# Sliding-window attention and MLP, two layers on one core: 164 pairs of operations on VectorE and GpSimd are put in a fixed order by semaphore waits

## The chip, the core and the metric

The kernel runs on one core of a Trainium2 chip. The core has TensorE (PE, matrix products into PSUM), VectorE (DVE), ScalarE (ACT), GpSimd (POOL) and SyncE (SP, which issues the transfers). Each engine has its own list of instructions and works through it in order; engines meet only through semaphores. [...] The metric is the time of one execution on the device, in microseconds (us).

## The reference

`x` holds 2048 rows of 512 numbers in bfloat16. Two kinds of block alternate, A, B, A, B, and both layers use the same weights:

```python
def _A_ref(x, wqkv, wo):          # 32 heads of 16, window of 256
    qkv = (x @ wqkv) ...          # q, k, v
    scores = einsum("bhqd,bhkd->bhqk", q, k) * Dh ** -0.5
    mask = (i - j >= 0) & (i - j < 256)
    p = softmax(where(mask, scores, -1e9))
    return einsum("bhqk,bhkd->bhqd", p, v) ... @ wo
def _B_ref(x, w1, b1, w2, b2):    # 512 -> 1792 -> 512
    return gelu(x @ w1 + b1) @ w2 + b2
x = x + _A_ref(_layernorm(x), A_wqkv, A_wo)
x = x + _B_ref(_layernorm(x), B_w1, B_b1, B_w2, B_b2)
x = x + _A_ref(_layernorm(x), A_wqkv, A_wo)
x = x + _B_ref(_layernorm(x), B_w1, B_b1, B_w2, B_b2)
```

## The kernel before

**Tiles and blocks.** `x` stays in SBUF as 16 tiles of 128 rows (`X`). The work of a layer is cut into 8 blocks of 256 rows, so blocks 0 to 7 are the first layer and 8 to 15 the second. Work of several blocks and of both kinds is interleaved: while one block's attention runs, the next blocks' projections and an earlier block's MLP run in between.

**Per block.** `layernorm` (from line 586) takes statistics on DVE (L591, L593), adds epsilon (L597) and raises to the power -1/2 on POOL (L603, with the constant `mhalf`, L512); `transposed` normalises on DVE (L613, `xn`) and transposes by a transfer or on PE (L625). `lnq` and `kv` project to Q, K and V (PE L639); the results are copied out of PSUM on DVE or ACT (L580, L582; K with a parity mask at L673). `attention` (from line 716) goes through 5 or 10 visits. A visit computes scores on PE (L740), takes exponentials on ACT (L747, two per visit, 128x1024 each), and multiplies one to two stretches of them by a 0/1 mask (`mask`, L768), on DVE or on POOL. `pv` multiplies by V on PE (L792), twice a block; DVE then transposes (L801), takes reciprocals (L805), divides (L809, on DVE or POOL) and transposes back (L815). `outproj` is PE L639 with `Wo_sb` and the addition to `X` on DVE (L841). `mlp` is W1 and W2 on PE (L639), bias and GELU on DVE and ACT (L864, L867, L872), the sum `X + b2` on POOL (L880, `Xb`) and the last addition on DVE (L884), whose rows are stored in the second layer. The constant masks are made at the start by POOL (L518 to L526).

**The order.** The program is first collected as 3080 operations, numbered as they are created (`_Plan.add`). `_ORDER` (line 167) is a table of these numbers: the one sequence in which all operations are emitted, so that each engine gets its part of that sequence in order. `_ALT` (line 323) lists the 154 operations that take their second choice of engine (a mask on POOL in place of DVE, for example), `_BANKS` (line 341) the PSUM banks. `_Plan.run` (line 390) walks `_ORDER`.

**The waits.** `_Sched.op` (line 62) turns what an operation reads and writes into waits: for each name read it needs the last writer's count, for each name written also the readers'. `_acquire` (line 44) drops a wait that the engine already knows to be met, by its own earlier waits or by what the engines it waited for had themselves waited for. Nothing in it orders two operations that touch no common name.

**Numbers of operations that the text below uses**, by engine, with the block they belong to:

- 60: DVE, epsilon for tile 0 (L597); 3: POOL, the constant `mhalf` (L512); 10: POOL, a constant mask (L521); 64: DVE, normalisation of tile 0 (L613)
- 201, 215: POOL, masks of block 0, visits 1 and 3; 369: DVE, mask of block 1, visit 0; 330: DVE, normalisation of tile 7
- 570: POOL, mask of block 2, visit 1; 420: DVE, the softmax division of block 1, second half (L809)
- 975: POOL, mask of block 4, visit 6; 957: DVE, mask of block 4, visit 3; 1095: POOL, mask of block 5, visit 6; 1077: DVE, mask of block 5, visit 3
- 1440: POOL, mask of block 7, visit 0; 1401: DVE, normalisation of tile 19
- 1477, 1486: DVE, masks of block 7, visits 7 and 9; 1487: POOL, mask of block 7, visit 9; 1753: DVE, normalisation of tile 23; 1705: POOL, mask of block 8, visit 2; 1701: DVE, mask of block 8, visit 1
- 1805: DVE, mask of block 9, visit 3; 1811: POOL, mask of block 9, visit 4; 2794: DVE, the division of block 14, first half; 2808: POOL, mask of block 14, visit 7

Of the kernel before, what the change touches and what calls it, by code (L numbers as in the profile page):

```python
# [19 lines left out]
class _Sched:  # L20
# [132 lines left out]
    def emit(self):  # L153
        nc = self.nc
        with nc.Block() as block:
            for eng in self.ENGINES:
                prog = self.prog[eng]
                if not prog:
                    continue

                def run(e, _prog=prog):
                    for cl in _prog:
                        cl(e)

                block._start_engine(run, _ENG_TYPES[eng])
# [173 lines left out]
]  # L339

_BANKS = [
# [20 lines left out]
class _Plan:  # L362
# [27 lines left out]
    def run(self):  # L390
        nodes = self.nodes
        assert sorted(_ORDER) == list(range(len(nodes)))
        for i in _ALT:
            nodes[i]["eng"], nodes[i]["fn"] = nodes[i]["alts"][1]
        banks = iter(_BANKS)
        free = set(range(8))
        seen = set()
        self.gmap = gmap = {}
        for i in _ORDER:
            nd = nodes[i]  # L400
            assert nd["deps"] <= seen
            seen.add(i)
            for g, k in nd["alloc"]:
                b = next(banks)
                gmap[g] = tuple(range(b, b + k))
                assert free.issuperset(gmap[g])
                free.difference_update(gmap[g])
            for g in nd["free"]:
                free.update(gmap[g])
        return _ORDER  # L410
# [545 lines left out]
```

## Time and profile before

| | us |
|---|---|
| median of 3 runs | 451.94 |
| lowest and highest | 451.18 and 452.74 |
| the profiled execution's own time | 451.18 |
| its span in the profile | 449.4 |
| granted TensorE clock in it | 1.0 |

The profile gives times from the start of the span. In the timeline's rows the first number is the start of an instruction, the second its length (of a group of equal ones in a row, their common length), then engine, line, operation, what it writes and reads, the shape and the count; in brackets the idle time of the engine before it and what ended that. In the table of waits a row names engine and line, what it waited for, and the total, the count and the longest. In a list by line the row ends with the busy time, the mean length in ns, and the engine's idle time before. In the view of one line the three numbers after the colon are the shortest, median and longest length in ns.

### The profile page before, as it was taken

The numbers are of one execution on the slowest core, as the hardware profiler recorded it, in microseconds if no ns is written. First come the engines' busy times: TensorE is split into PE (matmuls) and PEld (weight loads), VectorE is DVE, ScalarE is ACT, GpSimd is POOL, SyncE is SP. The second block draws the span as 40 slices with busy tenths as digits, with TensorE's granted clock in tenths as the row PEclk, the third lists the DMA queues.
The fourth block names the chain that finished last, engine by engine and source line by source line (L and its number), as shares of the span: only waits on it lengthen the run. The fifth ranks groups of instructions, "written<-read, shape, count | busy, mean of one in ns | idle before, by whom it ended". The sixth has DMA issues, their size and how long they took to land.

```text
span 449.4 us, 16895 instructions
## 1 busy us (share of the span) xinstructions
PE 425.1 (95%) x7579; PEld 230.9 (51%) x7579; DVE 356.1 (79%) x656; ACT 387.8 (86%) x458; POOL 190.8 (42%) x214
## 2 busy tenths in 40 slices
PE   8988999998799987999989999999999999999997
PEld 4555655645444543555445554555554553544763
DVE  6999867899796799976798689788787769855861
ACT  2999888998999898799989988898997989898732
POOL 5362343245452535456774323752337144314120
PEclk9999999999999999999999999999999999999999
DMA  8673721113211102201031301020431022102100
GB/s 248 187 175 85 207 39 31 26 32 45 49 24 25 26 2 39 64 21 29 4 68 27 42 15 26 10 43 20 57 85 39 1 32 70 36 1 50 39 23 25
DMA packets 47972, 23.25 MB, mean 52 GB/s; under 512 B 33180, under 2 KB 47900, under 8 KB 47900
## 3 DMA queue, kind: packets, MB, share of 16 engines
q1 hardware_dynamic: 47900, 22.17, 22.3%
q8 instruction: 60, 0.98, 0.9%
q14 instruction: 12, 0.10, 0.1%
HBM read 8.00 MB, written 2.10 MB: 22 GB/s over the span
## 4 chain that ended last, share of the span: by engine, by line
PE 75%; DVE 15%; ACT 7%; issue 1%; DMA 0%; POOL 0%; SPq 0%; DVEq 0%
PE ps L639 58%; PE ps L740 8%; PE ps L792 8%; ACT E L747 7%; DVE E L768 3%; DVE OD L801 2%; DVE KT L673 2%; DVE xn L613 2%; PE ps L532 1%; DVE stat L591 1%; DVE Va L580 1%; DVE OT L815 1%; DVE X L884 1%; DVE Nb L809 1%; DVE X L841 1%
## 5 line engine op out<-in xcount | busy, mean ns | idle before, releaser
L747 ACT ACTIVATE E<-ps 128x1024 bf16<-128x1024 f32 x300 | 284.3, 1038 | 31.8 <-PE ps L740 31.0
L768 POOL TENSOR_TENSOR E<-E,mask 128x512 bf16<-128x512 bf16 (+2 forms) x94 | 102.6, 1103 | 133.9 <-ACT E L747 133.8
L639 PE MATMUL ps<-W_sb,gT 128*128 128x512 bf16 x448 | 113.6, 380 | 0.0
L639 PE MATMUL ps<-xnTB,W_sb 128*128 128x512 bf16 (+1 forms) x560 | 110.8, 337 | 0.9 <-ACT E L747 0.9
L639 PEld LDWEIGHTS ps<-xnTB,W_sb 128*128 128x128 bf16 x560 | 51.9, 98 | 42.3 <-issue 2.8
L639 PE MATMUL ps<-xnTA,Wqkv_sb 128*128 128x256 bf16 x512 | 70.5, 273 | 3.3 <-DVE X L884 0.8
L740 PE MATMUL ps<-QT,KT 32*128 32x128 bf16 (+3 forms) x1920 | 60.9, 231 | 9.6 <-DVE X L841 2.1
L768 DVE TENSOR_TENSOR E<-E,mask 128x512 bf16<-128x512 bf16 (+2 forms) x142 | 65.1, 484 | 3.3 <-ACT E L747 2.9
L639 PEld LDWEIGHTS ps<-W_sb,gT 128*128 128x128 bf16 x448 | 39.6, 98 | 44.1 <-issue 4.0
L639 PEld LDWEIGHTS ps<-xnTA,Wqkv_sb 128*128 128x128 bf16 x512 | 46.6, 98 | 23.9 <-issue 4.3
L740 PEld LDWEIGHTS ps<-QT,KT 32*128 32x128 bf16 x1920 | 28.6, 92 | 57.7 <-ACT E L747 30.1
L872 ACT ACTIVATE gT<-ps,b1T 128x512 bf16<-128x512 f32 (+1 forms) x80 | 43.5, 605 | 11.3 <-PE ps L639 10.8
L801 DVE STREAM_TRANSPOSE OD<-ps 128x1024 f32<-128x1024 f32 x32 | 39.9, 1247 | 16.5 <-PE ps L792 16.1
L880 POOL TENSOR_TENSOR Xb<-X,b2all 128x512 f32<-128x512 bf16 x32 | 37.5, 1177 | 34.7 <-DVE X L884 34.6
L864 DVE TENSOR_SCALAR gT<-ps,b1T 128x512 bf16<-128x512 f32 (+1 forms) x60 | 36.8, 630 | 12.0 <-PE ps L639 11.5
L591 DVE BATCH_NORM_STATS2 stat<-X 128x6 f32<-128x512 bf16 x64 | 43.1, 682 | 2.6 <-DMA X<-in_A_x_dram 1.8
L673 DVE TENSOR_TENSOR KT<-ps,parmask 128x1024 bf16<-128x1024 f32 x32 | 38.8, 1214 | 7.7 <-PE ps L639 7.5
L792 PE MATMUL ps<-E,Va 64*17 64x64 bf16 (+3 forms) x1920 | 40.9, 230 | 3.1 <-DVE E L768 1.4
L792 PE MATMUL ps<-E,Vs 64*17 64x192 bf16 (+3 forms) x1920 | 41.6, 230 | 0.0
L639 PE MATMUL ps<-Wo_sb,OT 128*128 128x512 bf16 x128 | 37.3, 380 | 2.2 <-DVE OD L801 1.1
L613 DVE TENSOR_SCALAR xn<-X,statmv,rstd 128x512 bf16<-128x512 bf16 x64 | 32.1, 521 | 5.8 <-POOL rstd L603 5.1
L792 PEld LDWEIGHTS ps<-E,Va 64*17 64x17 bf16 x1920 | 29.3, 84 | 12.7 <-issue 6.3
(50 smaller groups left out, 350.4 us busy)
## 6 DMA issues: line engine op xcount, KB each, us to landing
Vs<-Va SPq DMA_DIRECT2D x64, 68.0 KB, 2.2
W_sb<-in_B_w_dram SPq DMA_DIRECT2D x4, 512.0 KB, 4.8
out_dram<-X SPq DMA_DIRECT2D x16, 128.0 KB, 1.9
X<-in_A_x_dram SPq DMA_DIRECT2D x3, 512.0 KB, 6.9
Wqkv_sb<-in_A_wqkv_dram SPq DMA_DIRECT2D x4, 256.0 KB, 4.5
W_sb<-in_B_w_dram SPq DMA_DIRECT2D x1, 768.0 KB, 4.9
W_sb<-in_B_w_dram SPq DMA_DIRECT2D x2, 384.0 KB, 3.5
Wqkv_sb<-in_A_wqkv_dram SPq DMA_DIRECT2D x1, 512.0 KB, 6.8
```

Of the source, the lines that this page charges most:

```text
L591: add("dve", lambda e, B, t=t, k6=k6: e.bn_stats(stat6[:, k6, :], X[:, t, :]), reads=["X%d" % t], writes=["st%d" % k6], key="bs%d" % (k + j))
L613: add("dve", lambda e, B: e.tensor_scalar(out=xn[:, s, :], in0=X[:, t, :], scalar1=statmv[:, k, 0:1], scalar2=rstd[:, k : k + 1], op0=ALU. ...
L639: r = e.matmul(ps[:, B[g][0], cols], lhsT, rhs, start=st, stop=sp)
L673: add("dve", lambda e, B, g=g, i=i: e.tensor_tensor(out=KT[:, kb, 2 * i : 2 * i + 2].rearrange("p c m a q -> p a (c m) q"), in0=ps[:, B[g] ...
L740: x = e.matmul(ps[:, bk[r], o : o + n], KT[rows, kb, c, m].rearrange("p a q -> p (a q)"), QT[rows, c, q : q + n], start=True, stop=True)
L747: add("act", lambda e, B, g_=g_, gi=gi: e.activation(E[:, 2 * gi : 2 * gi + 2, e0 : e0 + 512], ps[:, B[g_][0] : B[g_][0] + 2, :], AF.Exp, ...
L768: fn = lambda e, B: e.tensor_tensor(out=Ew, in0=Ew, in1=Mw, op=ALU.mult)
L792: x = e.matmul(ps[32 * r : 32 * r + VW, B[g][par], c % 2 * 2 * P + lo : c % 2 * 2 * P + hi], V[rows, (2 * b + m // 2) % VR, c * HC + 2 * r ...
L801: add("dve", lambda e, B: e.transpose(OD[:, s].rearrange("p a c q -> p (a c q)"), ps[:, B[g][0] : B[g][0] + 2, :]), reads=["ps:" + g], wri ...
L864: add("dve", lambda e, B, g=g, fc=fc: e.tensor_scalar(out=gT[:, fc, c0 : c0 + M], in0=ps[:, B[g][0], 0:M], scalar1=b1T[:, fc : fc + 1], sc ...
L872: add("act", lambda e, B, g=g, fc=fc: e.activation(gT[:, fc, c0 : c0 + M], ps[:, B[g][0], 0:M], AF.Gelu_apprx_tanh, bias=b1T[:, fc : fc + ...
L880: add("pool", lambda e, B, t=t, xs=xs: e.tensor_tensor(out=Xb[:, xs, :], in0=X[:, t, :], in1=b2all[:], op=ALU.add), reads=["X%d" % t, "b2a ...
```

## The change

A table `_TURNS` of 328 numbers is added, 164 pairs (a, z) one after the other; the reading "570, 420" is "operation 420 after operation 570". In each pair one operation is on DVE and the other on POOL: 87 times a is on POOL, 77 times on DVE, and a stands ahead of z in `_ORDER`. For each pair a name `turn<z>` is added to what a writes and to what z reads, so that `_Sched.op` makes z wait for a's count. `_ORDER`, `_ALT`, `_BANKS` and all operations stay as they were.

```diff
--- before.py
+++ after.py
@@ -338,6 +338,26 @@
     (1, -3, 1), (0, -3, 1), (1, -4, 1),
 ]
 
+_TURNS = [
+    13, 60, 60, 3, 60, 8, 60, 9, 60, 2, 10, 64, 64, 11, 11, 67, 11, 69, 12, 156, 201, 369, 201, 205, 206, 219, 215,
+    330, 330, 373, 387, 377, 387, 388, 388, 239, 415, 411, 411, 416, 525, 410, 570, 420, 570, 647, 306, 645, 598, 602,
+    598, 603, 503, 607, 503, 902, 904, 487, 904, 589, 589, 612, 589, 608, 589, 613, 617, 690, 690, 686, 686, 700, 686,
+    699, 695, 704, 704, 714, 704, 694, 704, 705, 718, 723, 718, 722, 728, 1020, 728, 727, 728, 732, 728, 733, 1024,
+    943, 737, 947, 975, 957, 975, 961, 864, 990, 864, 971, 989, 985, 989, 1063, 989, 848, 848, 966, 1071, 994, 1071,
+    832, 832, 1281, 832, 1279, 1076, 1010, 1076, 1082, 1076, 1081, 1081, 880, 1095, 1077, 1095, 1012, 1095, 1014,
+    1014, 1099, 1086, 1104, 1091, 1105, 1091, 1320, 1328, 1333, 1333, 1324, 1324, 1338, 1334, 1352, 1334, 1339, 1356,
+    1361, 1361, 1362, 1361, 1397, 1361, 1357, 1361, 1367, 1361, 1366, 1366, 1343, 1343, 1399, 1440, 1401, 1371, 1448,
+    1371, 1453, 1371, 1454, 1459, 1458, 1459, 1468, 1476, 1658, 1656, 1241, 1225, 1749, 1749, 1209, 1209, 1389, 1391,
+    1586, 1391, 1481, 1481, 1482, 1477, 1487, 1487, 1486, 1487, 1697, 1487, 1753, 1753, 1705, 1705, 1701, 1701, 1715,
+    1715, 1491, 1491, 1719, 1796, 1792, 1511, 1723, 1805, 1811, 1805, 1800, 1805, 1801, 1801, 1806, 1820, 1824, 1820,
+    1602, 1833, 1829, 1833, 1739, 1843, 2062, 2062, 2066, 2067, 1938, 1861, 1634, 2095, 2085, 1863, 2076, 2100, 2099,
+    2099, 2081, 2099, 2094, 2094, 2181, 2104, 2182, 2104, 2186, 2132, 2214, 2132, 2177, 2395, 1989, 2434, 2224, 2447,
+    2452, 2453, 2448, 2471, 2515, 2462, 2457, 2457, 2476, 2457, 2481, 2568, 2485, 2568, 2572, 2590, 2503, 2590, 2505,
+    2590, 2577, 2595, 2370, 2700, 2780, 2780, 2784, 2784, 2785, 2784, 2621, 2784, 2789, 2775, 2799, 2779, 2734, 2779,
+    2807, 2817, 2813, 2794, 2808, 2794, 2812, 2926, 2822, 2926, 2717, 2717, 2930, 2934, 2939, 2945, 2940, 2958, 2906,
+    2963, 2889,
+]
+
 _BANKS = [
     4, 7, 5, 1, 6, 0, 4, 6, 5, 0, 2, 4, 1, 2, 6, 0, 4, 6, 2, 1, 0, 2, 4, 6, 7, 0, 4, 0, 2, 6, 5, 6, 0, 4, 2, 0, 5, 4,
     0, 6, 2, 4, 0, 6, 4, 0, 2, 5, 7, 4, 0, 2, 6, 0, 5, 4, 6, 0, 5, 2, 6, 4, 0, 1, 4, 6, 0, 2, 1, 3, 5, 6, 7, 1, 5, 4,
@@ -392,6 +412,10 @@
         assert sorted(_ORDER) == list(range(len(nodes)))
         for i in _ALT:
             nodes[i]["eng"], nodes[i]["fn"] = nodes[i]["alts"][1]
+        for a, z in zip(_TURNS[0::2], _TURNS[1::2]):
+            nodes[a]["writes"] = nodes[a]["writes"] + ["turn%d" % z]
+            nodes[z]["reads"] = nodes[z]["reads"] + ["turn%d" % z]
+            nodes[z]["deps"].add(a)
         banks = iter(_BANKS)
         free = set(range(8))
         seen = set()
```

## The prediction

> **What bounds the kernel now.** I read the busy table, the chain that ended last and the table of waits first.
>
> ```profile
> PE 425.1 (95%) x7579; PEld 230.9 (51%) x7579; DVE 356.1 (79%) x656; ACT 387.8 (86%) x458; POOL 190.8 (42%) x214
> ...
> PE 75%; DVE 15%; ACT 7%; issue 1%; DMA 0%; POOL 0%; SPq 0%; DVEq 0%
> ...
> POOL E L768 <- ACT E L747: 133.8, 50, 9.3
> ```
>
> TensorE (PE) is busy for 425.1 of 449.4 us and is three quarters of the chain, so it idles 24.3 us in all, 5.4% of the span. It takes its instructions in order: a matmul whose operand is late holds up everything behind it. VectorE (DVE) is 15% of the chain. GpSimd (POOL) is no part of it; its masks mostly wait for ScalarE's exponentials (133.8 us).
>
> **The change part by part.** No operation is added, removed or moved between engines; a wait is put before an operation z of one engine for an operation a of the other. The scheduler leaves out a wait that its engine has already made (one entry with several followers waits once); following its bookkeeping through the table, 96 of the 164 remain, 47 on DVE and 49 on POOL. A wait whose a had ended before z began costs next to nothing. So I laid the pairs beside the timeline of the run before, operation by operation in program order on each engine. Of the 96, 46 had a finished in time. In 50, z began before a had ended, in most of them before a had even begun: 17 times it is DVE that now stands still for POOL, 33 times POOL for DVE. For each of these I took a's end, added 0.06 us for the signal (an estimate), ran the work queued behind z at its old durations, and looked for the first matmul in PE's order that needs one of those results; how late that matmul becomes is the price. Ten places carry most of it.
>
> Start, 2.1 us. Pairs 60→3 and 10→64.
>
> ```profile
> 2.61 0.40 POOL L512 MEMSET mhalf<- 128x2 f32 x1
> ...
> 4.14 0.57 POOL L603 TENSOR_TENSOR rstd<-rstd,mhalf 128x1 f32<-128x1 f32 x1 [0.77 <-DVE rstd L597]
> ...
> 5.89 0.24 POOL L521 TENSOR_SCALAR_AFFINE_SELECT mask<-mask 128x64 bf16<-128x64 bf16 x1
> ...
> 3.90 0.15 DVE L597 TENSOR_SCALAR rstd<-statmv 128x1 f32<-128x1 f32 x1
> ...
> 4.79 0.38 DVE L613 TENSOR_SCALAR xn<-X,statmv,rstd 128x512 bf16<-128x512 bf16 x1
> ...
> 7.92 0.27 PE L639 MATMUL ps<-xnTA,Wqkv_sb 128*128 128x256 bf16 x1
> ```
>
> POOL's constants must now wait for DVE's 3.90 (ends 4.05), so they go from 2.61 to 4.11, 1.50 late; POOL's own idle 0.77 swallows part, 0.73 stays. The first normalisation (4.79) must wait for the mask operation that ended at 6.13: 1.34 + 0.06 + 0.73 = 2.1 late. The second normalisation stands behind it, and the first projection (7.92) needs both.
>
> Blocks 0 and 1, 2.4 and 2.0 us. Pairs 201→369 and 215→330.
>
> ```profile
> 19.26 1.63 POOL L768 TENSOR_TENSOR E<-E,mask 128x768 bf16<-128x768 bf16 x1 [0.26 <-ACT E L747]
> ...
> 18.54 0.39 DVE L768 TENSOR_TENSOR E<-E,mask 128x512 bf16<-128x512 bf16 x1
> ...
> 20.72 0.26 PE L740 MATMUL ps<-QT,KT 32*128 32x192 bf16 x4 [0.23 <-DVE Va L580]
> ...
> 27.27 2.26 POOL L768 TENSOR_TENSOR E<-E,mask 128x512 bf16<-128x512 bf16 x2
> ...
> 26.36 0.40 DVE L613 TENSOR_SCALAR xn<-X,statmv,rstd 128x512 bf16<-128x512 bf16 x1
> ```
>
> The DVE mask at 18.54 waits to 20.95, 2.4 late; behind it stand the evacuations of K and V, and PE's scores at 20.72 were already released by that V. The normalisation at 26.36 waits for the first of two POOL masks (to about 28.4): 2.06, which the Q evacuations behind it hand to PE's next projection.
>
> Block 1 to 2, 4.4 us. Pair 570→420.
>
> ```profile
> 54.46 0.69 DVE L809 TENSOR_TENSOR Nb<-OD,Rc 128x512 bf16<-128x512 f32 x1
> ...
> 58.66 1.15 POOL L768 TENSOR_TENSOR E<-E,mask 128x512 bf16<-128x512 bf16 x1 [6.41 <-ACT E L747]
> ...
> 56.91 0.59 PE L639 MATMUL ps<-Wo_sb,OT 128*128 128x512 bf16 x2
> ```
>
> The softmax division at 54.46 must wait for a POOL mask that ends at 59.81, whose exponentials come later: 5.4 late. Division and transpose take 1.43 more, to 61.3; the output projection wanted them at 56.91.
>
> Blocks 4, 5 and 7: 2.8, 3.0 and 2.9 us. Pairs 975→957, 1095→1077 and 1440→1401.
>
> ```profile
> 118.44 0.95 DVE L768 TENSOR_TENSOR E<-E,mask 128x256 bf16<-128x256 bf16 x3
> ...
> 120.41 1.15 POOL L768 TENSOR_TENSOR E<-E,mask 128x512 bf16<-128x512 bf16 x1 [3.95 <-ACT E L747]
> ...
> 119.65 0.23 PE L792 MATMUL ps<-E,Va 64*17 64x128 bf16 x4 [0.61 <-DMA xnTB<-xn]
> ...
> 148.95 0.53 DVE L768 TENSOR_TENSOR E<-E,mask 128x256 bf16<-128x256 bf16 x1
> ...
> 150.70 1.16 POOL L768 TENSOR_TENSOR E<-E,mask 128x512 bf16<-128x512 bf16 x1 [1.38 <-ACT E L747]
> ...
> 149.57 0.23 PE L792 MATMUL ps<-E,Va 64*17 64x128 bf16 x4
> ...
> 183.30 0.31 DVE L613 TENSOR_SCALAR xn<-X,statmv,rstd 128x512 bf16<-128x512 bf16 x1
> ...
> 184.03 2.26 POOL L768 TENSOR_TENSOR E<-E,mask 128x512 bf16<-128x512 bf16 x2 [4.23 <-ACT E L747]
> ...
> 184.34 0.82 PE L639 MATMUL ps<-xnTB,W_sb 128*128 128x512 bf16 x3
> ```
>
> Each time DVE waits for a POOL mask of a later visit. Two masks start at 121.6 and end at 122.4, and P·V (119.65) needs them: 2.8. One ends at 152.5, P·V wanted it at 149.57: 3.0. At 183.30 the wait lasts to 186.36; behind it the bias addition that frees a bank for the third matmul of the row at 184.34 (at 184.57) ends at 187.4: 2.9.
>
> Blocks 7 and 8, 3.3 us, by three waits in a ring: 1477→1487→1486, 1753→1705, 1705→1701.
>
> ```profile
> 215.16 1.09 DVE L768 TENSOR_TENSOR E<-E,mask 128x256 bf16<-128x256 bf16 x3
> ...
> 213.40 1.64 POOL L768 TENSOR_TENSOR E<-E,mask 128x768 bf16<-128x768 bf16 x1 [2.01 <-ACT E L747]
> ...
> 217.06 1.64 POOL L768 TENSOR_TENSOR E<-E,mask 128x768 bf16<-128x768 bf16 x1 [2.03 <-ACT E L747]
> ...
> 218.50 0.34 PE L740 MATMUL ps<-QT,KT 32*128 32x192 bf16 x6
> ```
>
> POOL's 213.40 waits for the first DVE mask of 215.16 (to 215.44) and ends at 217.1; the next DVE masks wait for that and end with a normalisation at 218.5; POOL's 217.06 waits for that to 220.2; a DVE mask waits again, and the addition behind it, which frees the scores' bank, ends near 221.8, not before 218.50. Had only the last wait counted it would be 1.6.
>
> Blocks 9 and 14: 3.6 and 2.8 us, POOL waiting for DVE. Pairs 1805→1811 and 2794→2808.
>
> ```profile
> 236.52 0.62 DVE L768 TENSOR_TENSOR E<-E,mask 128x512 bf16<-128x512 bf16 x2
> ...
> 230.36 3.46 POOL L768 TENSOR_TENSOR E<-E,mask 128x768 bf16<-128x768 bf16 x3
> ...
> 237.31 0.23 PE L792 MATMUL ps<-E,Va 64*17 64x128 bf16 x4
> ...
> 389.34 0.69 DVE L809 TENSOR_TENSOR Nb<-OD,Rc 128x512 bf16<-128x512 f32 x1
> ...
> 382.32 3.70 POOL L768 TENSOR_TENSOR E<-E,mask 128x512 bf16<-128x512 bf16 x4
> ...
> 389.19 0.23 PE L792 MATMUL ps<-E,Va 64*17 64x128 bf16 x4
> ```
>
> Three POOL masks, done by 233.8 before, may now start at 237.0 and end at 240.5; DVE's second mask waits for them, and P·V at 237.31 is 3.6 late. The last two of the four POOL masks of 382.32 wait for the division that ends at 390.03, and end at 391.9: 2.8.
>
> Seven smaller places (1.5 at 193, 1.05 at 278, and five under 0.7) add 4.4, an estimate by the same reading. The sum is 2.1+2.4+2.0+4.4+2.8+3.0+2.9+3.3+3.6+2.8+4.4 = 33.7 us of lateness at PE.
>
> From it go two things. PE's old idle time behind such a stall is partly used up by it: 5.4% of some 10 us (ten exponentials' length, a choice) behind each of 12 larger places is 6.5 us. Bounds: nothing, or all of PE's 24.3. And DVE operations that POOL had held up now go first.
>
> ```profile
> L768 DVE TENSOR_TENSOR E<-E,mask x142: 228/419/2000, 16.9 to 419.9; 128x512 bf16<-128x512 bf16 x62, 128x768 bf16<-128x768 bf16 x50, 128x256 bf16<-128x256 bf16 x30
> ...
> L613 DVE TENSOR_SCALAR xn<-X,statmv,rstd 128x512 bf16<-128x512 bf16 x64 | 32.1, 521 | 5.8 <-POOL rstd L603 5.1
> ```
>
> A normalisation takes 0.40 at 26.36 and 0.52 in the mean: 64 × 0.12 = 7.7 us of blocking. Masks range up to 2.00 against a median of 0.42; I put them at as much again, an estimate, so 16 us of DVE time, of which DVE's 15% of the chain makes 2.4 us. Bounds: nothing, or all 16. Forecast: 33.7 − 6.5 − 2.4 = 24.8 us on a span of 449.4, or 474.2, and with the 1.8 that lie outside it (451.18 − 449.4) 476. The profiled execution is 0.8 below the median of 451.94, within what follows.
>
> [...]
>
> **The rivals.** (1) The cover is far larger: every idle us of PE is used up, 33.7 − 24.3 = 9.4, so 461. For it: DVE idles 93 us, time in which it can catch up. Against it: the stalls come where DVE ran without a gap, and ACT, fed by PE's scores, moves along with PE. (2) The waits feed each other as at 215, where the ring made 3.3 of 1.6. Five more such rings, 5 × 1.7, and no cover: 33.7 + 8.5 = 42, so 493. For it: 46 waits had slack that a shift can eat. (3) Faster: the lost time is DVE's blocking, and the waits end it while the stalls fall into DVE's idle time. If DVE's blocking in front of the P·V matmuls were all on the path, −16, so 435; with half, 443. It decides only if the first matmuls behind the stalls had about 3 us of slack each; the rows above show none to 0.6. (4) No change: the waited-for operations come earlier once all run in the table's order, and nothing binds, 451. Against it: their starts were set by ACT's exponentials, which no wait advances.
>
> **How the numbers follow.** Forecast 0.50 (its own range 468 to 483), rival 1 0.27, rival 2 0.15, rival 3 0.04, rival 4 0.04. The range 458 to 489 takes in rival 1 and part of rival 2. Faster by over 0.3% (what a measurement here can tell from no change) 0.04, within it 0.04, slower 0.92.
>
> **What would show it.** PE's busy time should stay near 425 while its idle time doubles. DVE should show idle time ended by POOL masks, near 3 us at each place, the longest some 5 us before a division (L809); POOL's masks should show waits ended by DVE. The output projection near 57 should start about 4 us later against the scores before it. The first projection should start near 10.0. DVE's normalisation should fall towards 0.40 in the mean. If PE's idle time stays at 24, the reading of the pairs is wrong; if DVE's idle grows but PE's does not, the cover is.

## The result: 8.7% slower, and the profile after

| | before | after |
|---|---|---|
| median of the runs, us | 451.73 (4 runs) | 491.44 (4 runs, 490.56 to 491.79) |
| ratio to before, 95% interval | | 1.0873 [1.0849, 1.0898] |
| profiled execution, us | 451.18 | 491.42 |
| its span, us | 449.4 | 489.6 |
| granted TensorE clock, mean | 1.0 | 0.961 |

The time moved the way that was forecast, by 39.7 us where 24.8 were forecast, and lies 2.4 us above the range. These are the busy table, the row of TensorE's clock over 40 slices, and the chain that ended last, from the page of the changed kernel (the table of 20 lines and the four lines that read it move the line numbers behind them by 24: L768 of before is L792):

```profile
PE 438.4 (90%) x7579; PEld 235.1 (48%) x7579; DVE 345.2 (71%) x656; ACT 388.5 (79%) x458; POOL 189.8 (39%) x214
...
PEclk9979979999989989989979899999999999999999
...
PE 65%; DVE 15%; ACT 9%; POOL 6%; issue 2%; DMA 1%; SPq 0%; DVEq 0%; POOLq 0%
...
L637 DVE TENSOR_SCALAR xn<-X,statmv,rstd 128x512 bf16<-128x512 bf16 x64 | 24.6, 405 | 16.3 <-POOL E L792 7.0
```

Four things are to be seen here. PE's idle time (span less busy) went from 24.3 to 51.2 us, 26.9 more, near the forecast's 24.8 for the whole change. But the same 7579 matmuls are also busy for 13.3 us longer (438.4 against 425.1), and 26.9 + 13.3 is the whole difference of the spans, 40.2. In the clock row seven slices show 7 or 8, where before shows 9 in every one:

```profile
PEclk9999999999999999999999999999999999999999
```

And the normalisation on DVE fell from 521 to 405 ns in the mean, as the prediction said; its longest took 1.72 us before (at 230.47, beside a POOL mask from 230.36 to 232.04) and takes 0.49 now. DVE is busy for 10.9 us less altogether.

The table of waits of the changed kernel (engine and line, what it waited for, total, count, longest) shows both new kinds:

```profile
POOL E L792 <- DVE E L792: 62.5, 16, 8.1
...
DVE E L792 <- POOL E L792: 18.1, 9, 3.5
```

Place by place the traces are compared by the operations on PE, which come in the same order in both: the end of one in the changed kernel less its end before is its lag, and a jump in the lag from one operation to the next is a stall.

| place (operation) | end before | end after | forecast | jump |
|---|---|---|---|---|
| first projection (its start) | 7.92 | 9.45 | 2.1 | 1.5 |
| scores of block 0, visit 4 | 21.12 | 25.41 | 2.4 | 2.7 |
| Q projection of block 2 | 28.16 | 34.94 | 2.0 | 1.0 |
| output projection, tile 2 | 57.51 | 69.78 | 4.4 | 5.5 |
| P·V, block 4, first half | 121.12 | 138.21 | 2.8 | 3.2 |
| P·V, block 5, first half | 150.94 | 171.52 | 3.0 | 2.8 |
| W1 of the fourth MLP job | 185.16 | 207.50 | 2.9 | 2.7 |
| scores of block 8, visit 4 (the ring) | 218.90 | 247.88 | 3.3 | 3.3 |
| P·V, block 9, first half | 238.74 | 272.67 | 3.6 | 4.5 |
| P·V, block 14, second half | 390.55 | 430.09 | 2.8 | 4.1 |

Ten places were named and ten are there. (At the last two the P·V itself ran at half clock for about 1 us of the jump: the idle times ahead of it are 3.55 and 3.09.) The longest, near 57 us in before, in the timeline of the changed kernel:

```profile
65.56 1.15 POOL L792 TENSOR_TENSOR E<-E,mask 128x512 bf16<-128x512 bf16 x1 [6.10 <-ACT E L771]
66.67 1.15 POOL L904 TENSOR_TENSOR Xb<-X,b2all 128x512 f32<-128x512 bf16 x1
...
66.82 1.55 DVE L833 TENSOR_TENSOR Nb<-OD,Rc 128x512 bf16<-128x512 f32 x1 [5.45 <-POOL E L792]
...
69.17 1.03 PE L663 MATMUL ps<-Wo_sb,OT 128*128 128x512 bf16 x2 [5.07 <-DVE OT L839]
70.00 2.80 PE L663 MATMUL ps<-W_sb,gT 128*128 128x512 bf16 x7
```

DVE's division stands 5.45 us for the POOL mask (forecast 5.4). Then it takes 1.55 us, not 0.69: when the mask ends POOL goes on to its next operation (66.67 to 67.82), and the division (66.82 to 68.37) runs beside that; the 0.69 in before had no POOL operation beside it. That adds 0.9. PE stands 5.07 us, and the seven matmuls behind take 2.80 us; in before the same seven took 1.67:

```profile
57.56 1.67 PE L639 MATMUL ps<-W_sb,gT 128*128 128x512 bf16 x7
```

The view by stretches of the changed kernel shows why (start and end, length, busy time and count for PE, its weight loads, DVE, ACT and POOL, then the granted clock):

```profile
64.60:69.00 4.40, 0.00 (x0) 0.00 (x0) 2.15 (x2) 0.89 (x1) 3.44 (x3) 0.60 0.00 0
69.00:72.30 3.30, 3.13 (x8) 1.19 (x9) 2.74 (x6) 0.00 (x0) 0.38 (x1) 0.51 0.18 36
```

In the stall the clock falls, and it stays at half for 3.1 us after PE has work again (69.17 to 72.26). The clock records of this trace hold eight such stretches inside the program, each 3.413 or 6.827 us long and 37.5 us together, one behind each of eight stalls of 2.3 us or more; behind stalls of 1.8 us and less there is none. Before had none.

### The profile page after: what moved, and what is told of

It reads as the page before. It is cut to its first block, busy times and chain, and to the rows that moved or that the text cites. A ratio compares the mean times of both kernels' runs of the same rounds, so it can differ in the third digit from the quotient of the medians.

```text
span 489.6 us, 16934 instructions
## 1 busy us (share of the span) xinstructions
PE 438.4 (90%) x7579; PEld 235.1 (48%) x7579; DVE 345.2 (71%) x656; ACT 388.5 (79%) x458; POOL 189.8 (39%) x214
## 4 chain that ended last, share of the span: by engine, by line
PE 65%; DVE 15%; ACT 9%; POOL 6%; issue 2%; DMA 1%; SPq 0%; DVEq 0%; POOLq 0%
PE ps L663 49%; PE ps L816 8%; ACT E L771 8%; PE ps L764 7%; POOL E L792 5%; DVE E L792 4%; DVE KT L697 2%; DVE OD L825 2%; DVE stat L615 1%; DVE X L908 1%; DVE xn L637 1%; DVE Nb L833 1%; DVE QT L604 1%; DVE OT L839 1%; DVE gT L888 1%
## 5 line engine op out<-in xcount | busy, mean ns | idle before, releaser
L792 POOL TENSOR_TENSOR E<-E,mask 128x512 bf16<-128x512 bf16 (+2 forms) x94 | 102.0, 1097 | 171.8 <-ACT E L771 95.7
L663 PE MATMUL ps<-W_sb,gT 128*128 128x512 bf16 x448 | 117.1, 389 | 0.0
L663 PE MATMUL ps<-xnTB,W_sb 128*128 128x512 bf16 (+1 forms) x560 | 113.6, 342 | 3.3 <-DVE gT L888 2.7
L792 DVE TENSOR_TENSOR E<-E,mask 128x512 bf16<-128x512 bf16 (+2 forms) x142 | 60.1, 448 | 26.8 <-POOL E L792 18.1
L663 PE MATMUL ps<-xnTA,Wqkv_sb 128*128 128x256 bf16 x512 | 72.7, 279 | 3.2 <-DVE Va L604 1.0
L764 PE MATMUL ps<-QT,KT 32*128 32x128 bf16 (+3 forms) x1920 | 62.7, 237 | 10.6 <-DVE Va L604 2.7
L816 PE MATMUL ps<-E,Va 64*17 64x256 bf16 (+3 forms) x1920 | 44.0, 241 | 20.8 <-DVE E L792 6.6
L764 PEld LDWEIGHTS ps<-QT,KT 32*128 32x128 bf16 x1920 | 29.3, 94 | 60.5 <-ACT E L771 26.2
L896 ACT ACTIVATE gT<-ps,b1T 128x512 bf16<-128x512 f32 (+1 forms) x80 | 43.9, 606 | 15.2 <-PE ps L663 14.9
L816 PEld LDWEIGHTS ps<-E,Va 64*17 64x17 bf16 x1920 | 30.8, 88 | 31.3 <-issue 17.9
L816 PE MATMUL ps<-E,Vs 64*17 64x256 bf16 (+3 forms) x1920 | 44.7, 242 | 0.0
L663 PE MATMUL ps<-Wo_sb,OT 128*128 128x512 bf16 x128 | 38.5, 388 | 6.4 <-DVE OT L839 5.1
L637 DVE TENSOR_SCALAR xn<-X,statmv,rstd 128x512 bf16<-128x512 bf16 x64 | 24.6, 405 | 16.3 <-POOL E L792 7.0
```

Source lines behind the costliest of these rows:

```text
L637: add("dve", lambda e, B: e.tensor_scalar(out=xn[:, s, :], in0=X[:, t, :], scalar1=statmv[:, k, 0:1], scalar2=rstd[:, k : k + 1], op0=ALU. ...
L663: r = e.matmul(ps[:, B[g][0], cols], lhsT, rhs, start=st, stop=sp)
L764: x = e.matmul(ps[:, bk[r], o : o + n], KT[rows, kb, c, m].rearrange("p a q -> p (a q)"), QT[rows, c, q : q + n], start=True, stop=True)
L792: fn = lambda e, B: e.tensor_tensor(out=Ew, in0=Ew, in1=Mw, op=ALU.mult)
L816: x = e.matmul(ps[32 * r : 32 * r + VW, B[g][par], c % 2 * 2 * P + lo : c % 2 * 2 * P + hi], V[rows, (2 * b + m // 2) % VR, c * HC + 2 * r ...
L896: add("act", lambda e, B, g=g, fc=fc: e.activation(gT[:, fc, c0 : c0 + M], ps[:, B[g][0], 0:M], AF.Gelu_apprx_tanh, bias=b1T[:, fc : fc + ...
```

## The experiments

All times are medians of several runs beside the kernel before on the same chip; the number behind is the difference from before in those runs. Each kernel is the changed one with another table `_TURNS`.

**Which pairs cost.** The 164 pairs were split by the profile of before: 98 in which a had ended when z began, 66 in which it had not.

```diff
-_TURNS = [ all 164 pairs ]
+_TURNS = [ the 98 pairs with a finished in time ]
```

> Only the 98 pairs whose first operation had ended before the second began in the profile of before. Theory (the cost is the matmuls that the late pairs hold up, plus the TensorE clock that drops behind such stalls): these waits cost nothing, 451 to 453 us. Rival (each wait has a price of its own, 39.7 us over the 96 waits that are emitted, 0.41 us each): some 46 waits, 19 us, so 471.

Measured 452.19 us, ratio 1.0003 [0.9991, 1.0016]: nothing, with the clock at 1.0 throughout. A wait that is already met is free here; the rival of a price per wait falls.

```diff
-_TURNS = [ all 164 pairs ]
+_TURNS = [ the other 66 pairs ]
```

> Only the 66 pairs whose first operation had not ended when the second began. Theory: the whole cost, 488 to 494 us. Rival (a price per wait): 50 of 96 waits, 21 us, so 473.

Measured 493.51 us, ratio 1.0911 [1.0868, 1.0954], 41.6 over. The whole cost sits in the late pairs. They were split again by the engine that waits.

```diff
+_TURNS = [ of the 66 late pairs the 21 with z on DVE ]
```

> Of the late pairs only the 21 in which VectorE waits for GpSimd. Theory (the stalls pass on whole and each of over some 2.5 us costs up to 3.4 us more by the halved clock): stalls of 2.4, 2.0, 4.4, 2.8, 3.0, 2.9, 1.6, 1.3 at the start and 2 us of small ones, 22 in all, and 1.5 us of clock behind five of them: 29.5, so 481, granted clock about 0.97. With the prediction's cover (a quarter of the stalls used up) and no clock: 17, so 469.

Measured 477.58 us (+25.7, ratio 1.0581 [1.0536, 1.0626]): between the two, nearer to the theory. The profiled execution took 481.26, at a granted clock of 0.974; the other three had 0.975 to 0.982.

```diff
+_TURNS = [ of the 66 late pairs the 45 with z on POOL ]
```

> Of the late pairs only the 45 in which GpSimd waits for VectorE. Theory: 3.2 and 2.8 us before P.V of blocks 9 and 14, 1.5 at 193, 0.7 at the start and 1.5 of small ones, 9.7 in all, and 1.5 us of clock behind two: 12.7, so 465. Together with the run of VectorE's waits 41 to 43 us over before if the places add up; rival (the waits feed each other): each set alone costs clearly less than its part, and the two together under 35.

Measured 464.52 us (+12.6, ratio 1.0267 [1.0228, 1.0307]), clock 0.988. The two sets make 38.3 of the 41.6. That lies between the 41 to 43 and the under 35 that were expected; the 3.3 that are missing are no more than the intervals of the three runs allow, so the places add up as far as this can tell.

The two sets differ in a way that neither theory had. I summed the jumps of the lag over 0.3 us by sign. With DVE's waits they are +24.4 and −0.4: almost nothing is made good. With POOL's waits they are +19.9 and −8.9: at some places PE comes sooner than before. (In these two traces 68 of the 7579 matmuls have no record, so the sums are good to some 0.7.) The whole change has −8.6.

**One stall by itself, and the clock.**

```diff
+_TURNS = [
+    570, 420,
+]
```

> Only the pair 570 before 420. Theory: a stall of 4.4 us at the output projection near 57 us, and behind it one or two windows of 3.4 us with the clock at half, worth up to 1.7 us each: 457 to 460. Rival without the clock: 4.4 us, 456, granted clock 1.0 throughout. Rival with cover (PE's idle time behind the stall is used up): under 4 us, below 455.5. Price per wait: 452.

Measured 458.85 us (+6.9, ratio 1.0139 [1.0123, 1.0155]). The timeline of that kernel:

```profile
62.01 1.03 PE L647 MATMUL ps<-Wo_sb,OT 128*128 128x512 bf16 x2 [5.23 <-DVE OT L823]
62.84 3.01 PE L647 MATMUL ps<-W_sb,gT 128*128 128x512 bf16 x7
```

The lag is −0.5 us ahead of the stall (operations differ by so much from one execution to another), 5.1 at its end and 6.6 after the slow matmuls: 5.6 of stall, 1.5 of clock. From there it is 6.60 or 6.61 for every attention, output and score operation from the next scores to 110 us, and 6.6 at the end. None of it is made good.

```diff
+_FILL = {424: (6, 22)}
...
+        def filler(e, bk, n):
+            for _ in range(n):
+                r = e.matmul(ps[:, bk, :], Wqkv_sb[:, 0, 0:P], Wqkv_sb[:, 0, 0:512], start=True, stop=True)
+            return r
...
+            if i in _FILL:
+                S_.op("pe", lambda e, f=_FILL[i]: filler(e, *f), reads=["Wqkv0_0", "Wqkv0_1"], writes=["bank%d" % _FILL[i][0]])
```

Here 22 matmuls of weights into a free bank, whose result nobody reads, stand ahead of operation 424, the held-up part of the output projection.

> The pair 570 before 420 again, and 22 matmuls (128x128 on 512 columns, of weights, into a free PSUM bank, never read) ahead of the held-up matmul of the output projection, so that TensorE works while it would stand still. Theory: the stall stays, the clock does not drop: 456, 1.5 to 3.5 us below the run with the pair alone. Rival (the clock plays no part): the same as the pair alone, or more by the matmuls' 4.7 us where they do not fit into the stall.

Measured 471.29 us (+19.4), a miss as a whole; but the place itself shows what was asked. The timeline of that kernel, matmuls there and weight loads further on:

```profile
57.95 4.91 PE L935 MATMUL ps<-Wqkv_sb 128*128 128x512 bf16 x22
63.03 0.61 PE L649 MATMUL ps<-Wo_sb,OT 128*128 128x512 bf16 x2 [0.17 <-DVE OT L825]
63.47 1.67 PE L649 MATMUL ps<-W_sb,gT 128*128 128x512 bf16 x7
...
115.86 0.09 PEld L802 LDWEIGHTS ps<-E,Vs 64*17 64x17 bf16 x2 [2.08 <-issue]
```

The wait is as long as before, PE works through it, the clock does not drop there, and the seven matmuls take 1.67 us again. The lag goes from 0.8 to 5.9 and stays there: 5.1 of stall, no clock. What was lost came later: from 114 us on PE stood 1.8 to 2.1 us at four places without a wait that the profile shows ("issue"), and two of these brought half-clock stretches of their own; elsewhere it lost about 1 us at a time. So the matmuls were run without the pair.

```diff
+_TURNS = [
+]
+_FILL = {424: (6, 22)}
```

> No pair at all, only the 22 matmuls ahead of the output projection near 57 us. Theory (the run with pair and matmuls lost 12 us after 100 us because 44 more instructions on TensorE shift where its sequencer runs out of instructions): the matmuls' own 4.7 us, and again idle times of TensorE of about 2 us that nothing but issue ends, the first near P.V at 108: 465 to 472. Rival (those losses come of the pair's delay): 456.5.

Measured 472.44 us (+20.3, ratio 1.0439 [1.0387, 1.0490]). The weight loads in its timeline show the same idle time at the same P·V:

```profile
115.04 0.09 PEld L801 LDWEIGHTS ps<-E,Vs 64*17 64x17 bf16 x3 [2.23 <-issue]
```

So the later loss came with the added instructions, not with the wait. Filling the stalls was therefore not tried on the whole change.

**Do the waits feed each other?**

```diff
+_TURNS = [
+    1477, 1487, 1487, 1486, 1753, 1705, 1705, 1701,
+]
```

> Only the four pairs 1477-1487, 1487-1486, 1753-1705 and 1705-1701. As the prediction read them, each wait pushes the next: 3.3 us at the scores at 218.5, and with one window at half clock 1.5 more: 455 to 457. Without feeding only the last counts: 1.6, 453.5.

Measured 457.33 us (+5.4, ratio 1.0116 [1.0095, 1.0137]).

```diff
+_TURNS = [
+    1705, 1701,
+]
```

> Only the pair 1705-1701, the last wait of the ring. Theory: 1.6 us, a stall too short for the clock to drop, 453.5. If the ring is not what makes the stall, the same as with all four.

Measured 453.23 us (+1.3, ratio 1.0028 [1.0016, 1.0040]), clock 1.0. The scores at 218.50 of before in the timelines of the run with four pairs and of the run with the last alone:

```profile
223.42 0.40 PE L748 MATMUL ps<-QT,KT 32*128 32x192 bf16 x12 [3.19 <-DVE X L892]
```

```profile
219.93 0.40 PE L748 MATMUL ps<-QT,KT 32*128 32x192 bf16 x12 [1.46 <-DVE X L892]
```

The stalls were forecast as 3.3 and 1.6. The ring is real; the longer stall also takes 3.4 us of half clock with it, the shorter none.

**Where the jumps forward come from.** In 11 late pairs DVE's operation had been held up by the very POOL operation that now waits for it. One of them alone:

```diff
+_TURNS = [
+    387, 388,
+]
```

> Only the pair 387-388: GpSimd's mask, which began 0.08 us before VectorE's in the profile of before and held it up from 0.56 to 2.00 us, now waits for it. Theory (VectorE's lost port time lies on the path): the scores at 36.9, which wait for an addition behind that mask, come 1.3 us sooner and stay so: 450.6. Rival (such time is hidden, as the prediction took 85% of it to be): 451.7 to 451.9.

Measured 451.11 us against 452.07, ratio 0.9973 [0.9961, 0.9984]. The timeline of before, then of this kernel (two masks on DVE, POOL's mask, the addition, the scores):

```profile
33.44 2.31 DVE L768 TENSOR_TENSOR E<-E,mask 128x512 bf16<-128x512 bf16 x2
...
36.49 0.40 PE L740 MATMUL ps<-QT,KT 32*128 32x256 bf16 x8 [1.23 <-DVE X L841]
```

```profile
33.39 0.85 DVE L776 TENSOR_TENSOR E<-E,mask 128x512 bf16<-128x512 bf16 x2
...
34.39 1.64 POOL L776 TENSOR_TENSOR E<-E,mask 128x768 bf16<-128x768 bf16 x1 [3.78 <-DVE E L776]
...
35.14 0.40 PE L748 MATMUL ps<-QT,KT 32*128 32x256 bf16 x8
```

POOL goes second; DVE goes first, its two masks take 0.85 us in place of 2.31, and the scores that waited 1.23 us for it wait no more. The "port time" of the expectation is this lengthening; that a port is its cause was not shown. The lag falls by 1.3 us there. Of this 0.7 is lost again at the P·V behind the scores, which stands 0.70 us and begins at 36.23, just after POOL's mask ends at 36.03; a little later 0.5 comes back. The measured gain of 1.0 lies between the theory (1.3) and the rival (at most 0.2).

```diff
+_TURNS = [
+    387, 388, 598, 602, 904, 487, 1391, 1586, 1328, 1333, 1324, 1338, 1366, 1343, 1511, 1723, 2132, 2214, 2395, 1989,
+    2779, 2734,
+]
```

> Only 11 pairs of the table in which VectorE's operation was held up by the GpSimd operation that now waits for it; 10.5 us of VectorE's time. Theory: most of it is on the path, as the matmuls that came sooner by 8.9 us in the run with GpSimd's waits alone show, less what a delayed division costs at 229: 443 to 446. Rival (the prediction's 15%): 450.3. If GpSimd's delays of 0.5 to 1.4 us reach the path: above 452.

Measured 444.30 us (−7.8), ratio 0.9825 [0.9808, 0.9841]: faster than both kernels. From its page, the busy table, the chain and the normalisation:

```profile
PE 424.5 (96%) x7579; PEld 230.5 (52%) x7579; DVE 344.6 (78%) x656; ACT 387.4 (88%) x458; POOL 189.3 (43%) x214
...
PE 82%; DVE 7%; ACT 7%; DMA 1%; POOL 1%; issue 1%; DVEq 0%; SPq 0%
...
L622 DVE TENSOR_SCALAR xn<-X,statmv,rstd 128x512 bf16<-128x512 bf16 x64 | 26.0, 425 | 6.0 <-POOL rstd L612 5.5 <-DVE Va L589 0.4
```

PE's idle time is 17.6 us, 6.7 less than before, and DVE's share of the chain has halved, from 15 to 7%. The lag falls by over 0.3 us at ten operations; the whole change has its falls at the same ten and at two more.

```diff
+_TURNS = [
+    387, 388, 397, 411, 598, 602, 902, 487, 904, 589, 1328, 1333, 1324, 1338, 1366, 1343, 1391, 1586, 1509, 1723,
+    1511, 1811, 2089, 2099, 2132, 2214, 2395, 1989, 2625, 2799, 2779, 2734,
+]
```

> 16 pairs, 5 of them new and 2 put elsewhere: wherever VectorE was held up by over 0.25 us in the profile of before, the GpSimd operation that held it waits; 13.3 us of VectorE's time. Theory: 440 to 444, below the run with 11 pairs. Rival: no better than with 11, since the added places lie where VectorE waits for TensorE anyway.

Measured 444.72 us, ratio 0.9827 [0.9809, 0.9844]: no better. Why the five added pairs bring nothing was not settled.

## Why the prediction was wrong in size

- **That met waits cost nothing** was right (452.19), and so was the choice of the late pairs as the whole cost.
- **The stalls by place** were right: 1.0 to 5.5 us at the ten places of the table against 2.0 to 4.4 forecast, and 31.3 in sum against 29.3 (some of the jumps hold a little of the slow clock). The term was undersized where the released DVE operation runs beside POOL's next one (1.55 us in place of 0.69; 5.5 against 4.4 near 57), and for the smaller places: put at 4.4, they add some 8 us in jumps of over 0.3 outside the half-clock stretches. The largest of them, 1.8, is at the P·V near 37 of before, whose masks on POOL now wait for DVE; it takes back the 1.3 that the swap there wins.
- **The step that failed** is the sentence that PE's busy time should stay near 425. Every stall was priced by its length alone. Eight of them also halved the clock, and the matmuls behind ran slowly: 13.3 us more of busy time. Counted in another way, by the lag that grows inside the half-clock stretches, it is 11.0 us. Either is most of the 14.9 us by which the forecast fell short, and it was no term of the sum and no rival.
- **The cover of 6.5 us** does not exist. With the single pair the lag stays at 6.6 to the end; with DVE's waits only 0.4 is made good. A likely reason, not tested by itself: PE's old idle times are waits for engines that are themselves fed by PE, so they move along.
- **DVE's freed time** was undersized: 2.4 us were taken, 15% of 16. The 11 pairs give 7.8 us from 10.5 us of blocking in the trace (their operations' lengths in before less those after), three quarters. In the whole change 8.6 us come back, nearly all of it at the same operations. By chance the two deductions, 8.9 together, came to the same as this one, so that the idle time was forecast well (24.8 against 26.9) for reasons that were half wrong.
- **The rivals.** Rival 2 gave 493, near the time, but for another reason: rings exist (5.4 against 1.3), yet the two sets of late pairs add up within their spread, and the greater part of what the forecast lacked is the clock. Rival 3 named the real gain and its condition; alone it makes the kernel faster, and in this change the stalls outweigh it. With no cover, the freed time as measured and the clock, the sum is 33.7 − 8.6 + 11 to 13 = 36 to 38, against 39.7; the smaller places, some 3.5 us above what they were put at, cover the rest.

## What to carry to other kernels

A wait between two engines costs what the first matmul behind it loses, and in this kernel, which TensorE bounds, that loss stayed to the end (6.6 us behind the single pair). Price it by the length of the stall and reckon with slow matmuls behind it as well: here all eight stalls of 2.3 us or more in the changed kernel brought them, and none of 1.8 or less. An order from a plan should be laid beside the trace before it is enforced: of 164 pairs here 98 changed nothing, and most of the rest enforced an order that the chip had not run in. Where an operation takes longer beside one of another engine (here a DVE mask 2.00 us against a median of 0.42, a normalisation 1.72 against 0.41), let the one that holds up TensorE go first and the one with slack wait: the 11 such pairs of the table are worth 1.7%.

## What the hardware showed unexpectedly

- TensorE's clock is lost in stalls shorter than a half-clock stretch, and no single length decides. In the changed kernel 2.34 us was enough and 1.82 was not. The stall of 2.66 us at the P·V of block 5 brought a drop there and in the run of all late pairs, and none in the run of DVE's late waits, where one of 2.23 did. In the run with pair and added matmuls 1.84 was enough once.
- What went ahead of the drops can be read from the clock records. In the 14 traces (before, after, twelve experiments) 31 drops lie inside the program, and those of one trace lie whole multiples of 3.413 us apart. With each trace cut by that raster, TensorE stood idle for 1.70 to 3.41 us of the stretch just ahead of a drop; of some 1740 other stretches at full clock only six had that much (1.70 to 1.92). In these traces, then, a drop came behind 1.70 us or more of idle time in one such stretch, six cases apart. The 2.66 us that brought none fell on two stretches, 1.43 and 1.24 in each.
- In the changed kernel the clock stayed at half (0.5 in the records) for 3.413 or 6.827 us from the drop. Five of its eight drops fell in the stall itself, three 0.8 to 1.7 us behind its end; one drop cost about 0.5 to 2.5 us.
- 22 added matmuls (44 instructions with their weight loads) on TensorE cost 20.3 us where they themselves take 4.9: afterwards TensorE stood about 2 us at several places without a wait that the profile shows; the longest such time of the kernel before was 1.2. It came back in both runs with these instructions; that TensorE's sequencer ran out of instructions, as the expectation has it, was not shown.
- A DVE operation that a POOL operation released took longer beside POOL's next one: the division took 1.55 us in place of 0.69 in the changed kernel (`Xb` on POOL from 66.67 to 67.82) and in the run with the single pair (from 59.51 to 60.66).
